# Attention first, weight preparation in stages, and separate runs of experts for even and odd slots

## The chip, the cores and the metric

The kernel runs on one core of a Trainium2 chip. TensorE (PE, with its weight loads as PEld), VectorE (DVE), ScalarE (ACT), GpSimd (POOL) and SyncE (SP, which here only issues transfers) each run their own list of instructions in order and wait for each other by semaphores. A transfer waits in its issuing engine's list like any instruction. The metric is device time in microseconds (us).

## The reference

```python
def reference(x, weight, moe_*, moe2_*):
    # x 4 x 3584 x 192; weight 8 x 7
    w = softmax(weight, axis=-1)                       # seven taps for each of 8 heads
    x = causal_window_sum(x, w)                        # 24 columns a head -> 14336 x 192
    x = moe(x, w_gate, w1, w2)
    return moe2(x, w_gate, w_output_gate, w1, w2)

def moe(x, w_gate, w1, w2):                            # 8 experts, 192 -> 1024 -> 192
    logits = x @ w_gate
    e = argmax(logits, 1); g = softmax(logits)[row, e]
    for each expert: out[e == k] = g * (relu(x[e == k] @ w1[k]) @ w2[k])
```

moe2 is the same with one more factor a row, a sigmoid of x @ w_output_gate at the row's expert. Each row goes to one expert alone, so both layers sort the rows by expert.

## The kernel before

**Attention** (`conv`, L401) takes 128 tiles of 112 rows, four a step, in 32 steps. A step multiplies by a banded matrix (L434, PE), finds a power of two for each row and scales (L447 to L460, DVE), splits the row into two float16 halves (the `chl` tile: L468 on ACT, L469 and L470 on POOL), turns it (L487) for the gate logits (L499) and stores it in DRAM.

**Routing** (`routing`, L1294) takes the logits in groups of 16 tiles, mostly on DVE. After a first wave of groups (`WAVE`: four of eight in layer 1, five of eight in layer 2) it fixes the place of the rows so far (`wave1`), and after the last group that of the others (`wave2`). `Q0` says how many blocks of 128 rows the first wave supplies (42, which is 21 slots).

**Weights** are prepared by `preps` (L238): 8 experts x 2 halves x 2 layers are 32 units. A unit is loaded (L232, L233, L235), its largest magnitude taken by partition (L260, L263, L269), then over all partitions by one `partition_all_reduce` on POOL (L132), it is scaled and rounded on ACT (L295, L296), the remainder taken on POOL (L301, two instructions a unit), and both halves stored in DRAM by SP (L309, L310, L312). Layer 1's units wait for the order of the experts (`eid`), which is taken from the first `EARLY` groups, and stand in that order; no unit comes ahead of that.

**Slots** (`moe`, L1126): each layer has 63, of which 56 are for 256 rows and 7 for 128. A slot belongs to one expert. Its rows are gathered three slots ahead on POOL (L1068), turned by SP (L1076), multiplied by the first weights (L1167, 40 matmuls), passed through ReLU and split (L1169 on ACT, L1170 on DVE) and multiplied by the second weights (L1183, 48 matmuls). Layer 1 splits its result on POOL (`ehl`, L1204 and L1205), turns it (L1212), stores it and takes layer 2's logits (L1221). Layer 2 scatters its rows (L1253). Even and odd slots have a weight buffer each; a load (L1104 to L1107 and L1124) goes out only where the expert differs from the one two slots back. The slots stand in the order of the experts, and so both buffers take every expert in turn.

**The order of the work** is written out in `run` (L1335). Attention steps run alone until `ready` (L1315) finds the first slots' weights and places; the rest are called from the first slots. `Turn` (L1414) hands out routing and preparation in pieces: at points A and B of an attention step and, through `bg2`, of a slot. In one turn a unit is past its all-reduce and the one before it is scaled and has its remainder taken, right behind that all-reduce on POOL.

Of the kernel before, what the change touches and what calls it, by code (L numbers as in the profile page):

```python
# [9 lines left out]
F16 = mybir.dt.float16  # L10
# [21 lines left out]

Q0 = 42
ROUND = 1.5 * 2**23

WAVE = (4, 5)

EARLY = 3
FIRST = 2

PACE = (1, 3, 5, 7)

LEAD = 1

HURRY = 2.0
BUDGET = 1.8

SLOW = 8

GV0 = 4  # L50
GV1 = 4

XACT = 0
W1A = range(8)
NA = 2
LO = ((0, 0, 0, 0, 0, 0, 0, 0), (0, 0, 0, 0, 0, 0, 0, 0))
W2D = (0,)
B2 = 0.3
B3 = 0.1
U2 = 18  # L60
U3 = 62
SLOWS = range(14)
B5 = 0.3
B4 = 1.0
# [4 lines left out]
MODE = 1  # L69
GATE = 9  # L70
GB = 9
LAG = 0
TB = 2
PW1 = 1
PR = 1
PC = 0
Q1 = 0
Q2 = 1
QX = 0
Q2W = 0  # L80
AB = 1.0


class Kern:
    def __init__(self, ctx, tc, x, weight, g1, w11, w12, g2, go2, w21, w22, out):
# [14 lines left out]
        self.parts = 0, Q0 // NSUB, self.NP - 1, self.NS  # L100

        self.full = lambda groups: -(-(groups * JC * CT - E * (T - 1)) // T)
# [5 lines left out]
    def slot(self, u):  # L108


        m, s = divmod(u, self.NS)
        i = s - (self.NP - (E - 1))
        if i >= 0 and i % 2:
            return m, 2, 1 + i // 2, self.NP * NSUB + i // 2, 1
        s -= max(0, i) // 2
        w = max(k for k in range(3) if s >= self.parts[k])
        return m, w, s - self.parts[w], s * NSUB, NSUB
# [43 lines left out]
    def constants(self):  # L161
# [24 lines left out]

        self.run8 = cp.tile([P, E, JC], F32, name="run8")
# [33 lines left out]
    def prep_load(self, m, pos, half):  # L221
# [3 lines left out]
        r = self.wp.tile([P, self.H], F32, tag="r", name="wr")  # L225
        if m == 0:
            ev = nc.sync.value_load(self.eid[pos >= FIRST][0:1, pos : pos + 1], min_val=0, max_val=E - 1)
            w = w[bass.ds(ev, 1)].rearrange("a p f -> (a p) f")
        else:
            w = w[pos]  # L230
# [7 lines left out]
    def preps(self, todo):  # L238
# [6 lines left out]
        todo = [(m, pos, half) for m, pos in todo for half in range(2)]  # L245

        def known(n):
            return n < len(todo) and (todo[n][0] == 1 or (todo[n][1] >= FIRST) in self.eid and (todo[n][1] < GATE or not self.ahead or self.begun >= GB))

        def absmax(u):  # L250
            u.am = wp.tile([P, NA], F32, tag="am", name="wam")
            n = u.what[0] * E + u.what[1]
            u.act = u.what[2] == 0 and n in W1A
            u.max = u.what[2] == 0 or n in W2D
            if u.act:

                ca = H // NA
                for c in range(NA):
                    none = wp.tile([P, CH], F16, tag="none", name="none", bufs=1)
                    nc.scalar.activation(none[:, 0:ca], u.r[:, c * ca : (c + 1) * ca], AF.Abs, scale=2.0**-4, accum_out=u.am[:, c : c + 1])  # L260
            elif u.max:
                for c in range(NC):
                    nc.vector.tensor_reduce(u.am[:, c : c + 1], u.r[:, c * CH : (c + 1) * CH], axis=AX.X, op=ALU.max, apply_absolute_value=True)  # L263
                    yield 0.8
            else:

                for c in range(NC):
                    none = wp.tile([P, CH], F16, tag="none", name="none", bufs=1)
                    nc.scalar.activation(none, u.r[:, c * CH : (c + 1) * CH], AF.Abs, scale=2.0**-11, accum_out=u.am[:, c : c + 1])  # L269

        def scale(u):
            m, pos, half = u.what
            if u.act:
                t = wp.tile([P, 1], F32, tag="amx", name="amx")
                nc.vector.tensor_reduce(t, u.amr, axis=AX.X, op=ALU.max)
                u.amr = t
            else:
                nc.vector.tensor_tensor(u.amr[:, 0:1], u.amr[:, 0:1], u.amr[:, 1:2], ALU.max if u.max else ALU.add)
            s, e = self.pow2(wp, u.amr[:, 0:1], [P, 1], "ws")
            u.h = self.wh.tile([P, 2, H], F16, tag="h", name="wh")  # L280
            if half == 0:
                self.e1 = e
            else:

                nc.vector.tensor_scalar(self.wexp[m][:, pos : pos + 1], self.e1, e, 0.125, ALU.mult, ALU.mult)
            u.direct = LO[half][pos] if m == 0 else 0
            u.s = s

        def main(u, cs):
            for c in cs:  # L290
                q = slice(c * CH, (c + 1) * CH)
                if c < u.direct:
                    nc.scalar.mul(u.h[:, 0, q], u.r[:, q], u.s)
                    continue
# [3 lines left out]
        def rest(u):  # L298
            for c in range(u.direct, NC):
                q = slice(c * CH, (c + 1) * CH)  # L300
                nc.gpsimd.tensor_tensor(u.h[:, 1, q], u.r[:, q], u.h[:, 0, q], ALU.subtract)  # L301
            for c in range(u.direct):
                q = slice(c * CH, (c + 1) * CH)
                nc.vector.scalar_tensor_tensor(u.h[:, 1, q], in0=u.r[:, q], scalar=u.s, in1=u.h[:, 0, q], op0=ALU.mult, op1=ALU.subtract)
# [10 lines left out]
        n = 0  # L315
        new = one = two = None
        while n < len(todo) or new or one or two:
            if not (new or one or two):
                while not known(n):
                    yield "T"  # L320

            yield "A"
            if two:
                store(two)
# [1146 lines left out]
```

## Time and profile before

| | |
|---|---|
| Median of 3 runs | 1713.41 us (1707.09 to 1719.94) |
| Profiled execution | 1707.2 us, span 1705.3 us |
| Mean granted TensorE clock | 0.855 of full speed |
| PE busy | 1277.2 us (75%) |
| DVE busy | 879.8 us (52%) |
| POOL busy | 621.7 us (36%) |
| ACT busy | 553.0 us (32%) |
| DMA | 284.46 MB, mean 167 GB/s |

Times in the views count from the start of the span. Busy time is that of recorded instructions; register, semaphore, configuration and transfer-issuing instructions do not count. Idle time that a row shows as "issue" is time in which the engine waited for nothing that the profile shows. The slots of layer 1 begin at 292 us and those of layer 2 at about 1124 us; stages are told apart by these.

### The profile page before, as it was taken

The page shows a single profiled execution, that of the slowest core. Times are in us where ns is not written, and L with a number is a line of the kernel's source. Part 1 is how long each engine was busy: PE and PEld are TensorE (multiplying, and loading weights), DVE is VectorE, ACT ScalarE, POOL GpSimd, SP SyncE. Part 2 cuts the span into 40 slices and gives each one's busy share as a digit, 9 for nine tenths or more (in the row PEclk, how much of TensorE's full clock was granted, in tenths as well). Part 3 has the DMA queues.
Part 4 walks back from the last instruction along what each step waited for, and adds up shares of the span by engine and source line. Part 5 has one row for each costly group of instructions (what it writes and reads, how often), then busy time and mean ns, then how long its engine had stood idle before and what let it go on. Part 6 is the DMA issues. An engine that isn't in the chain of part 4 may idle for free. (4 is left out here: it accounts for less than half of the span.)

```text
span 1705.3 us, 35513 instructions
## 1 busy us (share of the span) xinstructions
PE 1277.2 (75%) x12456; PEld 1159.7 (68%) x12456; DVE 879.8 (52%) x2639; ACT 553.0 (32%) x989; POOL 621.7 (36%) x689
## 2 busy tenths in 40 slices
PE   2884241756479768868875779889999998989785
PEld 2874241645469657757765668778999998878675
DVE  3795212736547656555645376658755434333232
ACT  0444333333323233424332421232323333233232
POOL 2342233433333333434334242334444443333333
PEclk9675555777779979989988789999999999999988
DMA  3463453965488869777786589885555447876772
GB/s 98 135 155 90 137 138 99 207 174 140 138 183 211 200 181 232 169 196 199 190 196 173 135 223 197 197 197 129 160 147 146 127 109 193 211 200 185 196 206 73
DMA packets 321713, 284.46 MB, mean 167 GB/s; under 512 B 202131, under 2 KB 282188, under 8 KB 321533
## 3 DMA queue, kind: packets, MB, share of 16 engines
q1 hardware_dynamic: 301372, 245.81, 57.1%
q0 software_dynamic: 17136, 34.68, 8.4%
q8 instruction: 102, 1.67, 0.4%
q10 hardware_dynamic: 3024, 1.66, 0.4%
q14 instruction: 79, 0.64, 0.1%
HBM read 273.86 MB, written 60.32 MB: 196 GB/s over the span
## 5 line engine op out<-in xcount | busy, mean ns | idle before, releaser
L1167 PEld LDWEIGHTS <-wb 128*128 128x128 f16 x4840 | 484.3, 105 | 283.0 <-DMA wb<-wda 134.0
L1183 PE MATMUL py<-wb,h 128*128 128x192 f16 x5592 | 498.8, 250 | 52.9 <-DMA wb<-wd 15.4
L1183 PEld LDWEIGHTS <-h 128*128 128x128 f16 x5592 | 476.5, 100 | 64.7 <-issue 41.6
L1167 PE MATMUL ph<-mxt,wb 128*128 128x256 f16 (+1 forms) x2950 | 380.8, 288 | 124.8 <-DMA wb<-wda 90.2
L1170 DVE SCALAR_TENSOR_TENSOR h<-ph,h 128x512 f16<-128x512 f32 x289 | 192.5, 687 | 297.6 <-ACT h L1169 271.5
L1167 PE MATMUL xp<-mxt,wb 128*128 128x256 f16 (+1 forms) x1890 | 247.9, 289 | 58.7 <-DMA wb<-wda 38.6
L1068 POOL DMA_INDIRECT row<-rec,idx x238 | 240.7, 1012 | 69.2 <-issue 50.0
L1253 POOL DMA_INDIRECT out_dram<-o,io x119 | 123.9, 1041 | 297.0 <-ACT h L1169 69.5
L1170 DVE SCALAR_TENSOR_TENSOR h<-xp,h 128x512 f16<-128x512 f32 x187 | 125.7, 687 | 168.1 <-ACT h L1169 143.6
L1169 ACT ACTIVATE h<-ph 128x512 f16<-128x512 f32 x289 | 165.6, 596 | 127.8 <-PE ph L1167 98.2
L301 POOL TENSOR_TENSOR wh<-wr,wh 128x768 f16<-128x768 f32 x64 | 105.6, 1664 | 242.3 <-issue 193.8
L1203 ACT CAST ehl<-exs 128x384 f16<-128x384 f32 (+1 forms) x63 | 31.0, 491 | 349.2 <-DMA rec<-ehl 216.7
L1169 ACT ACTIVATE h<-xp 128x512 f16<-128x512 f32 x187 | 108.9, 596 | 82.2 <-PE xp L1167 56.9
L295 ACT ACTIVATE wr<-wr,wss 128x768 f32<-128x768 f32 x64 | 59.6, 931 | 212.5 <-DVE wss L126 208.0
L1252 ACT ACTIVATE o<-py,sc 128x192 f32<-128x192 f32 x119 | 43.9, 417 | 238.9 <-PE py L1183 130.7
L1204 POOL TENSOR_TENSOR ehl<-exs,ehl 128x256 f16<-128x256 f32 (+1 forms) x63 | 44.0, 698 | 154.1 <-ACT ehl L1203 148.4
L499 PE MATMUL lg<-gawt,cxt 128*112 128x16 f16 x384 | 32.7, 219 | 74.1 <-DVE L L514 49.5
L499 PEld LDWEIGHTS <-cxt 128*112 128x112 f16 x384 | 32.7, 177 | 75.5 <-issue 35.9
L434 PE MATMUL ph<-x,tz 118*112 118x96 f32 x240 | 42.1, 347 | 54.0 <-DMA tz<-td 29.2
L434 PEld LDWEIGHTS ph<-x,tz 118*112 118x112 f32 x240 | 38.0, 251 | 55.9 <-issue 31.5
L434 PE MATMUL xp<-x,tz 118*112 118x96 f32 x272 | 45.4, 345 | 40.5 <-DVE cxs L460 37.0
L434 PEld LDWEIGHTS xp<-x,tz 118*112 118x112 f32 x272 | 42.6, 254 | 41.7 <-DVE cxs L460 37.8
(214 smaller groups left out, 1163.8 us busy)
## 6 DMA issues: line engine op xcount, KB each, us to landing
wb<-wd SPq DMA_DIRECT2D x125, 768.0 KB
wb<-wda SPq DMA_DIRECT2D x125, 512.0 KB
wb<-wdb SPq DMA_DIRECT2D x125, 256.0 KB
wb<-wdb SPq DMA_DIRECT2D x125, 128.0 KB
wr<-in_moe_w_dram SPq DMA_DIRECT2D x16, 768.0 KB
wd<-wh SPq DMA_DIRECT2D x16, 768.0 KB
rec<-chl SPq DMA_DIRECT2D x32, 336.0 KB
rec<-ehl SPq DMA_DIRECT2D x56, 192.0 KB
```

The costliest lines, as they stand in the source:

```text
L295: nc.scalar.mul(u.r[:, q], u.r[:, q], u.s)
L301: nc.gpsimd.tensor_tensor(u.h[:, 1, q], u.r[:, q], u.h[:, 0, q], ALU.subtract)
L434: nc.tensor.matmul(xp[:, :, hh * GD : (hh + 1) * GD], lhsT=self.tz[: self.KI, h, :], rhs=xin[b0][: self.KI, o : o + G, h * GD : (h + 1) * GD],
L499: nc.tensor.matmul(lg[:CT, g, :], lhsT=xt[:, g * 3 + b, :], rhs=self.ga[0][:, 1 if b == 1 else 0].rearrange("p a e -> p (a e)"), start=b == 0,
L1068: nc.gpsimd.indirect_dma_start(out=rw[:, :], out_offset=None, in_=rec[:, :], in_offset=bass.IndirectOffsetOnAxis(ap=idx, axis=0))
L1167: nc.tensor.matmul(ph[:, k, :], lhsT=l, rhs=xt[:, xb, 0:n], start=i == 0, stop=i == 4)
L1169: nc.scalar.activation(hi, ph, AF.Relu)
L1170: nc.vector.scalar_tensor_tensor(lo, in0=ph, scalar=0.0, in1=hi, op0=ALU.max, op1=ALU.subtract)
L1183: nc.tensor.matmul(py[:, c, 0:D], lhsT=h[:, f, a, c * P : (c + 1) * P], rhs=w[:, b, f, :], start=n == 0, stop=n == 3 * NCH - 1)
L1204: nc.gpsimd.tensor_tensor(hl[:, :, D + DB : 2 * D], xs[:, :, 0:P], hl[:, :, 0:P], ALU.subtract)
L1252: nc.scalar.activation(o, py[:, c, 0:D], AF.Copy, scale=sc)
L1253: nc.gpsimd.indirect_dma_start(out=self.out[:, :], out_offset=bass.IndirectOffsetOnAxis(ap=io[:, 0:1], axis=0), in_=o, in_offset=None, bou ...
```

## The change

All 32 attention steps now stand ahead of the first slot (`run` calls `conv` to its end). `WAVE` becomes (6, 5), `EARLY` 4, and `Q0` has a value for each layer: 40 and 56 blocks, 20 and 28 slots. A unit of preparation goes through stages a turn apart: load, one turn of nothing, magnitude, all-reduce and scale factor, rounding and remainder, store; several units are on their way at once. Up to six units of layer 2 go first, while the order of layer 1's experts is not known. `PACE` sets how many turns lie between units. From layer 1's second wave on, and in both waves of layer 2, the even slots take one half of the list of slots and the odd slots the other half (`woven`), so that each buffer goes through its own run of experts; layer 1's first 20 slots stay in the experts' order. The blocks' numbers come from a table `number` instead of a plain count. Transposes of attention tiles are all made by PE, and layer 1's stores all go out from SP.

```diff
--- before.py
+++ after.py
-Q0 = 42
...
-WAVE = (4, 5)
...
-EARLY = 3
-FIRST = 2
...
-PACE = (1, 3, 5, 7)
...
+Q0 = (40, 56)
+
+WAVE = (6, 5)
+
+EARLY = 4
+
+
+PACE = (3, 2, 1, 3)
+
+AHEAD = 6
+
+LA = 2
+
+RAWS = 4
...
+WORK = (0.9, 4.0, 2.2, 0.6)
+FIRST = 20
...
+        last = self.NP - 1
+        ones = list(range(self.NP, self.NS))
+        n = Q0[0] // NSUB
+        mid = (n + last) // 2 + 3
+        odd = list(range(mid, last))
+        for k, at in enumerate((0, 5, 9, 13)):
+            odd.insert(at + k, ones[k])
+        first = list(range(n)) + self.woven(range(n, mid), odd + [last] + ones[4:])
+        n = Q0[1] // NSUB
+        mid = (n + last) // 2 + 3
+        odd = list(range(mid, last))
+        for k, at in enumerate((0, 5, 10)):
+            odd.insert(at + k, ones[1 + k])
+        second = self.woven(range(n // 2), range(n // 2, n)) + self.woven(list(range(n, mid)) + ones[0:1], odd + [last] + ones[4:])
+        self.seq = [self.laid(m, order) for m, order in enumerate((first, second))]
...
+    def woven(a, b):
+        a, b = list(a), list(b)
+        while len(a) > len(b) + 1:
+            b.append(a.pop())
+        while len(b) > len(a):
+            a.append(b.pop())
+        return [x for i in range(len(a)) for x in (a[i : i + 1] + b[i : i + 1])]
...
+        stages = [(load, None)] + [(None, None)] * (LA - 1) + [(absmax, None), (allmax, scale), (main, rest), (store, None)]
+        held = LA + 3
+        self.e1 = [None, None]
+        units, gap = [], 0
+        while any(todo) or units:
             yield "A"
-            if two:
-                store(two)
-            if one:
-                scale(one)
-                if MODE == 0:
-                    main(one, range(NC))
-                elif MODE == 1:
-                    main(one, range(1))
-                yield 0.5
-            if new:
-                yield from absmax(new)
-            yield "B"
-            if one and MODE:
-                main(one, range(1 if MODE == 1 else 0, NC))
-            if new:
-                new.amr = self.allmax(wp, new.am if new.act else new.am[:, 0:NC], NA if new.act else NC, "amr" + "a" * new.act)
-            if one:
-                rest(one)
-            two, one, new = one, new, None
-            if known(n):
-                new = type("Unit", (), {})()
-                new.what = todo[n]
-                new.r = self.prep_load(*todo[n])
-                n += 1
-                if (new.what[0] == 1 and 2 * new.what[1] + new.what[2] in SLOWS) or (new.what[1] >= SLOW and new.what[2]):
-
-                    yield "A"
+            gap -= 1
+
+            m = 0 if todo[0] and self.eid is not None and len(todo[1]) % 2 == 0 else 1
+            more = todo[m] and (m == 0 or not todo[0] or len(todo[1]) > 2 * E - AHEAD or len(todo[1]) % 2)
+            if more and gap <= 0 and sum(u.stage < held for u in units) < RAWS:
+                u = type("Unit", (), {})()
+                u.what, u.stage = todo[m].pop(0), 0
+                units.append(u)
+                gap = PACE[(2 if self.attended else 0) + (m if self.attended else 1 - m)]
+            for point in range(2):
+                for u in units:
+                    do = stages[u.stage][point]
+                    if do:
+                        do(u)
+                        yield 0.2
+                if point == 0:
                     yield "B"
+            for u in units:
+                u.stage += 1
+            units = [u for u in units if u.stage < len(stages)]
...
-            q = k + 1 if self.ahead else k
-            if last < q < NG:
-                attend(q)
-                last = q
+            if k + 1 < NG:
+                attend(k + 1)
...
-            while not self.ready():
-                next(conv, None)
+            while next(conv, "end") != "end":
                 k += 1
                 if k in (8, 10, 12):
                     next(gb, None)
-            for _ in range(LEAD):
-                next(conv, None)
+                self.ready()
+            ctx.close()
+            while not self.ready():
+                bg("B")
+                bg("A")
...
             def bg2(u, point):
-                if point == "A" or u in PACE:
-                    next(conv, None)
                 work.tick("B")
-                work.run(0.5 if u < U2 else B3 if u < U3 else B5)
+                work.run(WORK[2 if u < FIRST else 3])
```

In the order of POOL, `ISA` at the all-reduce's line (L132; L145 in the change) and at the next instruction's line stand for the configuration of the engine, which goes before and after the all-reduce. The first place is attention, eight to ten steps from its beginning. Before, on POOL, steps without any unit (the row subtractions of two steps, and routing's product between them):

```order
L469 TENSOR_TENSOR chl<-cxs,chl 112x4x128
L470 TENSOR_TENSOR chl<-cxs,chl 112x4x64
L606 TENSOR_TENSOR d<-d,inv_110 112x128
L469 TENSOR_TENSOR chl<-cxs,chl 112x4x128
L470 TENSOR_TENSOR chl<-cxs,chl 112x4x64
```

Now, on POOL, the fourth to the seventh step, one unit in three steps:

```order
L145 ISA
L145 ISA amr<-wam 128x2
L477 ISA
L477 TENSOR_TENSOR chl<-cxs,chl 112x4x128
L478 TENSOR_TENSOR chl<-cxs,chl 112x4x64
L435 MEMSET x 6x192
L324 TENSOR_TENSOR wh<-wr,wh 128x768 x2
L477 TENSOR_TENSOR chl<-cxs,chl 112x4x128
L478 TENSOR_TENSOR chl<-cxs,chl 112x4x64
```

Ahead of the first gather of a slot's rows (the `row` tile) POOL had 6 units' all-reduces, 5 units' remainders and 26 steps; now it has 13, 12 and all 32. Of the 32 all-reduces 10 of layer 2's units and 9 of layer 1's stand behind it, where it was 26.

The second place is layer 1's slots, in the middle of the layer. Before, on POOL, two slots, each with its two gathers and the two subtractions of `ehl`; the all-reduce and, right behind it, the remainder `wh` of the unit before follow in the second:

```order
L1068 DMA row_4514<-rec_60,idx_0_2288 128x194
L1068 DMA row_4516<-rec_60,idx_0_2288 128x194
L1204 TENSOR_TENSOR ehl<-exs,ehl 128x2x128
L1205 TENSOR_TENSOR ehl<-exs,ehl 128x2x64
L1068 DMA row_4704<-rec_60,idx_0_2288 128x194
L1068 DMA row_4706<-rec_60,idx_0_2288 128x194
L1204 TENSOR_TENSOR ehl<-exs,ehl 128x2x128
L1205 TENSOR_TENSOR ehl<-exs,ehl 128x2x64
L132 ISA
L132 ISA amr<-wam 128x2
L301 ISA
L301 TENSOR_TENSOR wh<-wr,wh 128x768 x2
```

Now, on POOL, from the all-reduce in one slot to the remainder of the same unit in the next; a third slot without either follows:

```order
L145 ISA
L145 ISA amr<-wam 128x2
L1198 ISA
L1198 TENSOR_TENSOR ehl<-exs,ehl 128x2x128
L1199 TENSOR_TENSOR ehl<-exs,ehl 128x2x64
L1065 DMA row_6311<-rec_60,idx_40_5008 128x194
L1065 DMA row_6313<-rec_60,idx_40_5008 128x194
L1198 TENSOR_TENSOR ehl<-exs,ehl 128x2x128
L1199 TENSOR_TENSOR ehl<-exs,ehl 128x2x64
L324 TENSOR_TENSOR wh<-wr,wh 128x768 x2
```

So an all-reduce stood behind the slot's `ehl` and directly ahead of a remainder; now it stands ahead of the slot's `ehl`, and the remainder comes a slot later. In both, SP's store of a unit is the first thing in the slot behind the remainder, ahead of that slot's weight loads.

## Rows read from the trace of the kernel before

**Rows 1.** The page: span and number of instructions.
```profile
span 1705.3 us, 35513 instructions
```

**Rows 2.** Windows by stage: length, busy us (instructions) by engine, granted clock, DMA share, GB/s.
```profile
35.00:135.00 100.00, 80.06 (x744) 78.09 (x743) 87.09 (x232) 40.17 (x58) 38.05 (x48) 0.70 0.59 149
135.00:294.00 159.00, 52.74 (x426) 50.28 (x426) 49.02 (x184) 58.05 (x91) 41.21 (x42) 0.52 0.42 118
294.00:519.00 225.00, 145.36 (x1262) 126.32 (x1260) 118.83 (x312) 75.97 (x128) 78.67 (x82) 0.78 0.69 167
519.00:956.00 437.00, 341.17 (x3325) 301.37 (x3324) 249.38 (x716) 155.77 (x273) 158.31 (x184) 0.89 0.77 194
956.00:1124.00 168.00, 130.40 (x1365) 117.55 (x1363) 103.03 (x304) 40.51 (x78) 57.92 (x72) 0.86 0.85 190
1124.00:1443.00 319.00, 307.81 (x3169) 288.14 (x3167) 175.84 (x559) 104.21 (x214) 141.64 (x140) 1.00 0.57 146
1443.00:1705.00 262.00, 213.88 (x2150) 192.11 (x2148) 88.26 (x303) 76.20 (x149) 97.91 (x99) 0.93 0.69 181
```

**Rows 3.** The same windows for L1169 alone: four to a slot of 256 rows.
```profile
294.00:519.00 225.00, 26.62 (x49) 0.78 0.69 167
519.00:956.00 437.00, 74.02 (x137) 0.89 0.77 194
```

**Rows 4.** The same two windows for L132, the all-reduce of preparation.
```profile
294.00:519.00 225.00, 3.31 (x9) 0.78 0.69 167
519.00:956.00 437.00, 5.15 (x14) 0.89 0.77 194
```

**Rows 5.** Timeline of POOL, attention steps with preparation: start, length, instruction, [idle before].
```profile
141.66 0.37 POOL L132 PARTITION_ALL_REDUCE amra<-wam  x1 [7.13 <-ACT cxt L492]
156.85 0.37 POOL L132 PARTITION_ALL_REDUCE amr<-wam  x1 [6.12 <-issue]
164.51 3.23 POOL L301 TENSOR_TENSOR wh<-wr,wh 128x768 f16<-128x768 f32 x2 [7.30 <-ACT cxt L492]
251.09 1.30 POOL L1068 DMA_INDIRECT row<-rec,idx  x1 [0.19 <-issue]
286.93 0.37 POOL L132 PARTITION_ALL_REDUCE amr<-wam  x1 [7.60 <-issue]
```

**Rows 6.** Timeline of POOL, attention steps without preparation, and one all-reduce among them.
```profile
43.23 1.15 POOL L469 TENSOR_TENSOR chl<-cxs,chl 112x512 f16<-112x512 f32 x1 [2.12 <-ACT chl L468]
71.07 0.67 POOL L470 TENSOR_TENSOR chl<-cxs,chl 112x256 f16<-112x256 f32 x1
77.72 0.37 POOL L132 PARTITION_ALL_REDUCE gbamr<-gbam  x1 [5.98 <-DVE cat L450]
85.28 1.14 POOL L469 TENSOR_TENSOR chl<-cxs,chl 112x512 f16<-112x512 f32 x1 [7.19 <-issue]
125.22 1.16 POOL L469 TENSOR_TENSOR chl<-cxs,chl 112x512 f16<-112x512 f32 x1 [3.85 <-issue]
```

**Rows 7.** Waits of SP, first layer: who waited for whom, total, times, longest.
```profile
SPq L309 <- POOL wh L301: 72.2, 6, 17.4
SPq L312 <- POOL wh L301: 42.8, 5, 12.0
```

**Rows 8.** Waits of PE, first layer.
```profile
PE ph L1167 <- DMA wb<-wda: 83.1, 16, 12.7
```

**Rows 9.** Timeline of SP at one preparation store.
```profile
958.89 0.35 SPq L312 DMA_DIRECT2D wd<-wh  x1
960.29 0.34 SPq L1104 DMA_DIRECT2D wb<-wda  x1
```

**Rows 10.** Timeline of PE at the same place.
```profile
967.42 0.82 PE L1167 MATMUL xp<-mxt,wb 128*128 128x256 f16 x3 [10.78 <-DMA wb<-wda]
```

**Rows 11.** Lines of PE in 1124 to 1443 us: count | busy, mean ns | idle.
```profile
L1183 PE MATMUL py<-wb,h 128*128 128x192 f16 x1632 | 141.5, 246 | 4.4 <-issue 3.6 <-ACT o L1252 0.7
L1167 PE MATMUL ph<-mxt,wb 128*128 128x256 f16 x832 | 98.8, 273 | 5.1 <-DVE h L1170 1.9 <-DMA wb<-wdb 1.8 <-issue 1.2
```

## What the change is predicted to do

> **What bounds the kernel now.** The first view is the windows by stage: 135 us of attention at a good pace, 159 us in which attention goes on slowly, 830 us for the 63 slots of layer 1 and 581 us for the 63 of layer 2. The reader is to see that PE's share differs: 308 of 319 us in the first part of layer 2, 341 of 437 us in the middle of layer 1, and 53 of 159 us before it [rows 1, 2]. Only 1124 to 1443 us is bounded by PE: 36 slots, 8.9 us each, at the full granted clock of 2.4 GHz. Its matmuls give the same: 40 of 118.8 ns (98.8 us over 832) and 48 of 86.7 ns (141.5 over 1632) are 8.9 us [rows 2, 11].
>
> The second view is POOL's timeline, because POOL is called 36% busy and is not. An all-reduce is recorded with 0.37 us, but POOL stands still for some 6 us ahead of it and 7 us behind it: from 71.74 us (71.07 + 0.67) to 85.28 us, 13.5 us in all, and nothing in between but the all-reduce [rows 6]. A unit of preparation thus holds POOL for 13.5 + 3.2 (the two remainders) = 16.7 us. Where attention steps have a unit each, eight all-reduces start between 141.66 and 286.93 us, 20.75 us apart, while the steps without stand 5.1 us apart (the third at 43.23, the nineteenth at 125.22 us) [rows 5, 6].
>
> The third view is the waits of layer 1. SP waits 115 us for POOL's remainder before it can store a unit [rows 7]; the weight loads stand behind the store. At 958.89 us the store goes out, at 960.29 us the load, and PE, which has nothing to do meanwhile, starts at 967.42 us after 10.78 us of idling [rows 9, 10]. Such waits for first weights make 83.1 us on one of the two sets of banks alone [rows 8].
>
> **The change part by part.** The sum is made against the profiled execution's 1707.2 us (span 1705.3); the median, 1713.41, is 0.4% above it.
>
> *Attention and early units.* Work ahead of the first gather grows from 26 steps, 6 all-reduces and 5 units' remainders to 32, 13 and 12. POOL sets the pace: three steps with one unit are 16.7 + 3 x 1.8 = 22 us there, where DVE at 5.1 us a step needs 15. From the third step at 43 us five such groups end at 153 us. Then seven steps follow with one remaining unit to finish, some 42 us (35 at 5.1 us a step and half of an all-reduce): 195 us. The seventh to tenth all-reduces stand two steps apart, 20.3 us, 61 us in all; then one step, 18.5 us; then two without a step, 33.5 us; and the thirteenth's own 13.5 us: 322 us. Eight gathers of 1.3 us [rows 5], their turning and the first matmuls, 18 us: the first ReLU at 340 us instead of 294, **+46 us**. Below, POOL never idles and each all-reduce takes the shortest form, 5.98 + 0.37 + 6.5 us: 320 us, +26. Above, every unit's turn takes 20.75 us and 23 others 5: 43 + 270 + 115 + 18 = 446 us, +152. I stay near the POOL sum, since the one all-reduce among quick steps [rows 6] was followed by two row subtractions 1.7 us apart: the others had gone on and caught up. The longer tables (`number`) are made ahead of attention's first step on POOL, which waits for PE's banded matrix: 0, and if that cover were gone, a few us that the bounds hold. That PE gets 1.2 GHz in such a stretch, as it does in 135 to 294 us (granted 0.52) [rows 2], costs nothing: its 80.06 us for some 20 steps at 0.70 are 5.4 us a step at 0.52, and three of them still fit in 22 us.
>
> The Trainium skill (GPSIMD Engine Reference, section 2.1, Instruction dispatch) says that the first call to a freshly loaded kernel pays some 6 us of code loading that no instruction shows. The gap ahead of the all-reduce agrees (5.98 us), but the rows show a second, 7.2 us, on the way back. With 6.4 us an all-reduce, an estimate by that page, the front would be some 90 us shorter and the result about 1530; the rows decide.
>
> *Slots 0 to 11 of layer 1*, 225 us: nine all-reduces fall here [rows 4], and nine now. Six steps' row subtractions (11 us of POOL) go, and two of seven weight loads: **-15 us**. Bounds 0 and, if POOL alone counts (9 x 16.7 + 24 gathers of 1.3 us = 182 us), -43.
>
> *Slots 12 to 45*, 437 us [rows 2] with 137 ReLU instructions, four a slot, so 34 slots [rows 3]: 14 all-reduces before [rows 4], 10 now, because six units of layer 2 are already done; 21 weight loads before, 13 now. These loads I counted by going through both lists of slots with the experts that the reference gives each row (72 before in both layers, 51 now). Of the 34 slots three are now short. PE needs 31 x 8.9 + 3 x 4.45 = 289 us. The end of layer 2, which has many loads and no units, takes 251 us without its tail of 11 us, where its 20 long and 7 short slots need 209: 1.2 times. So 347 us, and 8 us for what the units still disturb, as their remainder and store now have a slot more: 355 us, **-82 us**. Above: now 134 us over PE's 303 are 9.6 us a unit; if a unit cost its whole 13.5 us, 289 + 135 = 424 us, -13. Below: 1.1 times PE's need, 318 us, -119.
>
> *Slots 46 to 62*, 168 us: 13 long and 4 short slots instead of 10 and 7, PE's need 133 us; by 1.2, 160 us, **-8 us** (0 to -22). The rest of the seven short slots lies in the stretch above.
>
> *Layer 2*, 581 us: 56 x 8.9 + 7 x 4.45 + 11 = 541 us, so 40 us are waits, nearly all after 1443 us, where 19 loads fall on 27 slots. Now 13 fall on the first 36 slots and 12 on the last 27. That is 0.44 a slot, as in the first 36 slots before (16 loads), which had no waits to speak of: **-35 us** (-10 to -40). Routing of the second wave ends by slot 20 in the order of DVE, ahead of its first use at slot 25; DVE was busy for 55% there (175.84 of 319 us), so it keeps up.
>
> Work moved between slots on ACT and DVE costs nothing: in slots 12 to 45 they are busy for 36% and 57% [rows 2]. With slots of 8.9 us DVE would be late next, where routing falls on it; the factor 1.2 holds room for that. DMA was busy for 336 us of slots 12 to 45 (0.77 of 437) [rows 2]; eight loads and four units less, some 7 us each (an estimate: what the 19 loads after 1443 us add to the share of layer 2's first 36 slots with 16), leave 250 of 355 us, so it does not become the bound.
>
> Sum: 46 - 15 - 82 - 8 - 35 = -94, so 1613 us, and 1620 on the scale of the median.
>
> **The rivals.**
> A. *Everything stands still at an all-reduce.* It now comes ahead of a slot's `ehl` instead of behind it, and SP's turning of `ehl` holds up the second weights and the row turns behind it. In the front the same happens to every turn. For: the 20.75 us turns of 141 to 287 us. Against: the quick recovery at 85 us, and that there each turn also waited for the unit before. Front +152, slots 12 to 45 at 424 us (-13), slots 0 to 11 at 0, the rest as forecast: 152 - 13 - 8 - 35 = +96, about 1809. It decides once the first slot begins after 434 us with the rest as forecast. Chance 0.09.
> B. *The units cease to matter.* Front +26, slots 0 to 11 -30, slots 12 to 45 -119, 46 to 62 -22, layer 2 -38: -183, about 1530. For: only half the unit's chain now lies in one slot. Against: 9.6 us a unit now. Chance 0.13.
> C. *The loads were not the point.* A unit goes on costing 9.6 us through the store's wait, 289 + 96 = 385 us (-52), slots 0 to 11 and 46 to 62 stay, layer 2 gains 10: 46 - 52 - 10 = -16, about 1697. For: 115 us of waits of SP for POOL. Chance 0.16.
>
> **How the numbers follow.** The forecast has 0.62. About 1% is what a measurement of this kernel tells from no change. Faster by more takes in the forecast (0.61), B and nearly half of C: 0.81. Within 1% lie the rest of C and a front halfway to A: 0.11. Slower: nearly all of A, 0.08. The range 1545 to 1705 leaves out A, most of B and C's upper tail, together 0.2.
>
> **What would show it.** Right: POOL's gaps of 6 and 7 us at each of 13 all-reduces ahead of the first slot, that slot's ReLU at 320 to 370 us; SP waiting far less than 115 us at the unit stores; layer 1 below 750 us; layer 2 at 535 to 560 us with PE at the full clock. Wrong: turns of 20 us in attention without a unit's end in them, DVE's `exs` waiting for POOL's `ehl`, or PE waiting as long for first weights as now.

## The result, and the profile after

The changed kernel takes 1638.03 us (median of 4 runs, 1628.8 to 1643.44), the kernel before 1716.6 us in the same comparison: ratio 0.9545, 95% interval 0.9485 to 0.9606. It is faster, 18 us above the 1620 that was forecast and inside the range.

The page of the changed kernel, its span and the busy time of its engines:

```profile
span 1634.9 us, 35772 instructions
PE 1258.3 (77%) x12560; PEld 1162.7 (71%) x12560; DVE 892.6 (55%) x2620; ACT 577.1 (35%) x1037; POOL 624.0 (38%) x709
```

Its windows by stage, columns as in [rows 2]. They are the front up to the first ReLU, slots 0 to 11, 12 to 45 and 46 to 62 of layer 1, and layer 2 in two parts:

```profile
0.00:359.00 359.00, 166.06 (x1407) 159.83 (x1408) 176.68 (x502) 141.24 (x213) 125.59 (x165) 0.62 0.50 133
359.00:562.00 203.00, 143.42 (x1223) 126.54 (x1222) 124.05 (x304) 72.94 (x126) 61.16 (x63) 0.82 0.53 137
562.00:917.00 355.00, 295.08 (x3112) 270.19 (x3112) 219.25 (x630) 141.24 (x258) 149.91 (x179) 0.93 0.78 184
917.00:1062.00 145.00, 135.30 (x1504) 127.29 (x1503) 110.67 (x324) 41.27 (x80) 51.18 (x66) 0.98 0.87 187
1062.00:1393.00 331.00, 315.48 (x3233) 293.21 (x3231) 177.29 (x566) 107.50 (x217) 140.31 (x142) 0.98 0.50 129
1393.00:1635.00 242.00, 202.95 (x2090) 185.60 (x2088) 84.68 (x296) 72.93 (x147) 95.88 (x97) 0.93 0.51 141
```

Read the second number of each row against [rows 2]. The front is 65 us longer; slots 0 to 11 take 203 us instead of 225, slots 12 to 45 take 355 instead of 437, slots 46 to 62 take 145 instead of 168, and layer 2 takes 573 instead of 581. PE's busy time fell by 19 us, from 1277.2 to 1258.3; the rest of the 70 us between the two spans is idle time of PE that went.

POOL's timeline of the changed kernel in the front (start, length, instruction, idle before it) shows why the front grew so far. What follows first is one all-reduce, then a later stretch with two in succession:

```profile
70.21 0.66 POOL L478 TENSOR_TENSOR chl<-cxs,chl 112x256 f16<-112x256 f32 x1
78.18 0.37 POOL L145 PARTITION_ALL_REDUCE amr<-wam  x1 [7.31 <-issue]
86.52 1.15 POOL L477 TENSOR_TENSOR chl<-cxs,chl 112x512 f16<-112x512 f32 x1 [7.97 <-PE lg L504]
...
94.79 0.66 POOL L478 TENSOR_TENSOR chl<-cxs,chl 112x256 f16<-112x256 f32 x1
103.68 0.37 POOL L145 PARTITION_ALL_REDUCE amr<-wam  x1 [8.23 <-DMA rec<-chl]
103.97 0.43 POOL L145 PARTITION_ALL_REDUCE gbamr<-gbam  x1
111.49 1.14 POOL L477 TENSOR_TENSOR chl<-cxs,chl 112x512 f16<-112x512 f32 x1 [7.10 <-ACT cxt L497]
```

From the end of the last subtraction to the next, an all-reduce holds POOL for 15.65 us (70.87 to 86.52), where [rows 6] had 13.5. Two back to back, 0.29 us apart, take 16.0 us together: the price is paid on the way in and on the way out, not by the reduction. From the first subtraction behind the first one (86.52) to the last one ahead of the next (95.45) POOL is never idle, so it does set the pace here.

The waits of the changed kernel in layer 1, 359 to 1062 us (who waited for whom, total, times, longest), first SP's, then PE's:

```profile
SPq L329 <- POOL wh L324: 58.5, 7, 14.0
SPq L332 <- POOL wh L324: 32.0, 4, 11.6
```

```profile
PE py L1180 <- issue: 28.3, 5, 9.3
PE ph L1164 <- DVE h L1167: 23.3, 5, 7.8
PE ph L1164 <- DMA wb<-wda: 11.5, 4, 4.6
```

PE's wait for first weights, 83.1 us in [rows 8], is down to 11.5, although SP still waits 90.5 us at the unit stores (115 in [rows 7]). Another wait of SP fell more. Ahead of a slot's weight loads SP also turns gathered rows, and in slots 12 to 62, where 60.6 of the 83.1 us lay, it waited for the gathers 92.5 us before (519 to 1123 us) and 15.6 us now (562 to 1062 us):

```profile
SPq L1076 <- DMA row<-rec,idx: 92.5, 18, 11.9
```

```profile
SPq L1073 <- DMA row<-rec,idx: 15.6, 10, 3.9
```

At the stores of the same slots it waited 33.9 us before and 25.3 now. PE's longest wait for first weights before, 12.7 us, is such a case. On POOL, SP and PE, one after the other:

```profile
607.27 0.37 POOL L132 PARTITION_ALL_REDUCE amr<-wam  x1 [7.61 <-issue]
615.45 3.24 POOL L301 TENSOR_TENSOR wh<-wr,wh 128x768 f16<-128x768 f32 x2 [7.81 <-issue]
618.87 1.19 POOL L1068 DMA_INDIRECT row<-rec,idx  x1 [0.18 <-issue]
```

```profile
621.68 2.49 SPq L1076 DMA_TRANSPOSE mxt<-row  x2
627.63 0.36 SPq L1104 DMA_DIRECT2D wb<-wda  x1
```

```profile
632.43 0.82 PE L1167 MATMUL ph<-mxt,wb 128*128 128x256 f16 x3 [12.74 <-DMA wb<-wda]
```

The gather stood behind the all-reduce and the remainder, SP's row turn behind the gather (11.9 us of waiting), the load behind the row turn. The change puts the gathers ahead of the all-reduce in POOL's list.

### The profile page after: what moved, and what is told of

The parts are those of the page before. It is cut to its first block, busy times and chain, and to the rows that moved or that the text cites. A ratio compares the mean times of both kernels' runs of the same rounds, so it can differ in the third digit from the quotient of the medians.

```text
span 1634.9 us, 35772 instructions
## 1 busy us (share of the span) xinstructions
PE 1258.3 (77%) x12560; PEld 1162.7 (71%) x12560; DVE 892.6 (55%) x2620; ACT 577.1 (35%) x1037; POOL 624.0 (38%) x709
## 5 line engine op out<-in xcount | busy, mean ns | idle before, releaser
L1164 PEld LDWEIGHTS <-wb 128*128 128x128 f16 x4840 | 470.2, 101 | 187.5 <-issue 70.3
L1164 PE MATMUL ph<-mxt,wb 128*128 128x256 f16 (+1 forms) x2970 | 357.1, 278 | 79.6 <-DVE h L1167 25.3
L1164 PE MATMUL xp<-mxt,wb 128*128 128x256 f16 (+1 forms) x1870 | 235.0, 281 | 33.2 <-DMA wb<-wda 12.0
L306 DVE TENSOR_REDUCE amx<-amr 128x1 f32<-128x2 f32 x32 | 5.0, 155 | 223.6 <-POOL amr L145 223.6
L145 POOL PARTITION_ALL_REDUCE amr<-wam x32 | 11.8, 368 | 227.3 <-issue 166.1
L446 PE MATMUL xp<-x,tz 118*112 118x96 f32 x256 | 49.5, 383 | 43.4 <-DVE cxs L470 40.0
L446 PEld LDWEIGHTS xp<-x,tz 118*112 118x112 f32 x256 | 46.2, 288 | 44.8 <-DVE cxs L470 41.2
```

The lines of the kernel that those rows point to most:

```text
L446: nc.tensor.matmul(xp[:, :, hh * GD : (hh + 1) * GD], lhsT=self.tz[: self.KI, h, :], rhs=xin[b0][: self.KI, o : o + G, h * GD : (h + 1) * GD],
L1164: nc.tensor.matmul(ph[:, k, :], lhsT=l, rhs=xt[:, xb, 0:n], start=i == 0, stop=i == 4)
```

## The experiments

The stages of each profiled run are told apart by the same ReLU instructions in all of them (us, good to about 1; layer 2 up to the span's end). They come from one execution each; e2's took 1647.6 us, 17 less than the median of its runs. The kernel before was run again beside each group of experiments, at medians of 1719.9 to 1722.6 us, and the ratios are to those:

| kernel | first ReLU | slots 0-11 | 12-62 | layer 2 | median, ratio to before [interval] |
|---|---|---|---|---|---|
| before | 294 | 225 | 605 | 581 | 1716.6 |
| changed | 359 | 203 | 500 | 573 | 1638.0, 0.9545 [0.9485, 0.9606] |
| e1 | 359 | 202 | 526 | 579 | 1662.7, 0.9640 [0.9578, 0.9702] |
| e2 | 291 | 205 | 575 | 575 | 1664.2, 0.9674 [0.9622, 0.9725] |
| e3 | 430 | 154 | 576 | 584 | 1746.0, 1.0144 [1.0091, 1.0198] |
| e4 | 263 | 174 | 480 | 570 | 1486.8, 0.8636 [0.8590, 0.8681] |
| e5 | 358 | 203 | 535 | 566 | 1657.7, 0.9626 [0.9574, 0.9678] |
| e6 | 297 | 203 | 528 | 565 | 1594.3, 0.9289 [0.9225, 0.9354] |
| e7 | 237 | 175 | 500 | 563 | 1479.9, 0.8606 [0.8550, 0.8661] |
| e8 | 281 | 172 | 469 | 564 | 1481.5, 0.8598 [0.8552, 0.8645] |
| e9 | 360 | 204 | 502 | 569 | 1633.0, 0.9463 [0.9423, 0.9503] |
| e10 | 361 | 203 | 512 | 571 | 1647.9, 0.9548 [0.9506, 0.9591] |
| e11 | 358 | 203 | 499 | 556 | 1620.6, 0.9415 [0.9366, 0.9463] |
| e12 | 237 | 175 | 505 | 575 | 1493.4, 0.8654 [0.8618, 0.8690] |

Where the order of layer 2's slots is that of the change and its loads are kept, layer 2 takes 563 to 575 us; a difference of a few us in one stage of one profile is within that scatter.

### e1: the changed kernel with the slots in the experts' order

```diff
-        self.seq = [self.laid(m, order) for m, order in enumerate((first, second))]
+        plain = list(range(self.NP - (E - 1)))
+        for k in range(E - 1):
+            plain += [self.NP - (E - 1) + k, ones[k]]
+        self.seq = [self.laid(m, order) for m, order in enumerate((plain, plain))]
```

> The changed kernel with both layers' slots in the plain order of the experts again (72 weight loads instead of 51), all else as changed. If fewer loads are a good part of the gain: layer 1 loses 20 to 40 us and the end of layer 2 some 20 us, so 1675 to 1700 us. If the loads were hidden once the units' stores no longer hold them up: 1638 us, within 8. If they were the whole gain: 1700 to 1720.

1662.7 us: between the cases. Separate runs of experts are worth 25 us of the 79 by the medians and 16 by the two ratios, whose intervals overlap a little; the profiles put 26 in slots 12 to 62 and 6 in layer 2. The rest of the gain is not in the order of the slots. PE's wait for first weights is as small here, with the loads that the kernel before has, as in the changed kernel (561 to 1087 us):

```profile
PE ph L1167 <- DMA wb<-wda: 11.4, 6, 3.4
```

### e2: the kernel before, remainder ahead of the all-reduce

```diff
             yield "B"
...
+            if one:
+                rest(one)
             if new:
                 new.amr = self.allmax(...)
-            if one:
-                rest(one)
```

> The kernel before with one thing moved: in a turn the remainder of the older unit goes out on POOL ahead of the all-reduce of the newer one, so the store a turn later does not stand behind 13.5 us of all-reduce. My theory (the store's wait holds up the weight loads of layer 1): SP's 115 us of waits for the remainder fall below 50, PE's waits for first weights by half, 1655 to 1680 us. The rival (a unit costs what it costs, wherever its remainder stands): 1705 to 1720.

1664.2 us from two lines that change places, inside the range of the theory. In its first layer's slots, 291 to 1071 us, SP waits for POOL's remainder at the stores and PE for the first weights like this:

```profile
SPq L312 <- POOL wh L301: 19.2, 3, 6.7
SPq L309 <- POOL wh L301: 17.0, 3, 6.6
```

```profile
PE ph L1167 <- DMA wb<-wda: 24.9, 9, 5.7
```

SP's 115 us of [rows 7] became 36, and PE's 83.1 us of [rows 8] became 24.9. That bears out the chain of rows 7, 9 and 10: remainder behind an all-reduce, store behind the remainder, load behind the store. But the two lines move more than the remainder. The gathers of the next slot now come straight behind the all-reduce, and the second gap stands behind them:

```profile
638.87 0.37 POOL L132 PARTITION_ALL_REDUCE amr<-wam  x1 [5.77 <-DMA rec<-ehl]
639.43 1.19 POOL L1068 DMA_INDIRECT row<-rec,idx  x1 [0.19 <-issue]
640.92 0.95 POOL L1068 DMA_INDIRECT row<-rec,idx  x1 [0.30 <-issue]
649.36 0.66 POOL L1204 TENSOR_TENSOR ehl<-exs,ehl 128x256 f16<-128x256 f32 x1 [7.50 <-issue]
```

So e2 takes the all-reduce with both gaps out ahead of the remainder, and the second gap out ahead of the gathers. In slots 12 to 62 SP's waits fell from 33.9 to 11.1 us at the stores and from 92.5 to 76.9 us for gathered rows. How the gain divides between the two branches no run shows.

### e3: the kernel before with all attention ahead of the slots

```diff
-LEAD = 1
+LEAD = 10
```

> The kernel before with ten more attention steps ahead of the first slot, so that all 32 precede the slots; preparation, waves and order of slots as before. My theory (attention ahead of the slots earns nothing by itself): the first ReLU 60 to 120 us later, layer 1 shorter by nearly as much, since the units of these turns are done, 1695 to 1735 us. The rival (attention in the slots was what made them slow): below 1690.

1746.0 us, 11 us above the range that was expected. Slots 0 to 11 lose 71 us and slots 12 to 62 lose 29, but the front grows by 136. By the trace it holds three steps more (ACT had split all 32 by the first ReLU, where it was 29) and seven more all-reduces (15 instead of 8). So this is attention moved ahead together with its units, all else as before, and it costs 1.4% (0.9 to 2.0). What attention alone would cost no run shows. The changed kernel's front is not the same one, since it has one unit in three steps at first and 13 in all.

### e4: the changed kernel without the preparation's all-reduces

The largest over the partitions becomes a mean, by a matmul with ones and a factor of 1/128. It goes out at point B, the scaling a turn later.

```diff
-            u.amr = self.allmax(wp, u.am, NC, "amr")
+            a16 = wp.tile([P, NC], F16, tag="a16", name="a16")
+            nc.vector.tensor_copy(a16, u.am)
+            ps = self.rps.tile([P, G, 2 * E], F32, tag="lg", name="aps")[:, 0, 0:NC]
+            nc.tensor.matmul(ps, lhsT=self.ones16, rhs=a16, start=True, stop=True)
+            u.amr = wp.tile([P, NC], F32, tag="amr", name="amr")
+            nc.vector.tensor_scalar(u.amr, ps, 1.0 / P, None, ALU.mult)
...
-        stages = ... [(absmax, None), (allmax, scale), (main, rest), (store, None)]
+        stages = ... [(absmax, None), (None, allmax), (scale_main, rest), (store, None)]
```

> The changed kernel with the 32 all-reduces of preparation taken from POOL: PE adds the 128 partitions' sums with a matrix of ones, DVE takes a 128th (the scale is then the mean over the partitions, where it was the largest). My theory (POOL stands still for 13.5 us at each all-reduce and sets the pace of the front and of slots 0 to 11): the first ReLU at 240 to 280 us instead of 359, slots 0 to 11 in 140 to 170 us instead of 203, 1470 to 1530 us. The rival (the unit's chain over DVE, ACT and SP sets the pace, POOL only lies beside it): above 1600.

1486.8 us, 151 less than the changed kernel and inside the theory's range; only slots 0 to 11, at 174 us, lie above its 140 to 170. 13 all-reduces stood in the front, 8 in slots 0 to 11 and 11 behind; the stages are shorter by 96, 29 and 20 us: 7.4, 3.6 and 1.8 us an all-reduce. (Against e5, which has the same stages, the last is 55 us, or 5.0 each.) POOL's busy time, by contrast, is 617.4 us on this kernel's page and 624.0 on that of the changed one: 6.6 us of busy time stood for 151.

The Trainium skill (GPSIMD Engine Reference, section 4.1, Engine selection) gives a reduction along the partitions to GpSimd. For 128 x 2 values between other work on POOL this case's runs speak against it: with a mean by TensorE in place of the largest value the kernel takes 151 us less, for 32 calls.

### e5: the changed kernel, all-reduce behind `ehl`

The stages of e4 with the all-reduce kept, and the scale factor half a turn later with it: the control for e4's layout, and a test of rival A.

```diff
-        stages = ... [(absmax, None), (allmax, scale), (main, rest), (store, None)]
+        stages = ... [(absmax, None), (None, allmax), (scale_main, rest), (store, None)]
```

> The changed kernel with its all-reduces kept, but each issued at point B of a turn (behind a slot's ehl on POOL) instead of point A, and the scale factor computed in the next turn: the stage layout of e4_sum_on_pe without its replacement of the all-reduces. If e4's 151 us come from the all-reduces themselves: 1638 us, between 1620 and 1655. If the layout did a good part of it: 1600 us or less. If an all-reduce ahead of ehl held up the slots (rival A's mechanism in small): layer 1's slots shorter by 10 to 30 us, 1608 to 1628, with the front unchanged.

1657.7 us, above every case: none had the layout as a loss. So e4's gain is not its layout (against this control it is 171 us). And the all-reduce costs more behind a slot's `ehl` than ahead of it: 20 us by the medians, with intervals that overlap, and 35 us in the profiles' slots 12 to 62 (e9 and e10 repeat this comparison). Rival A had it the other way round. ACT's waits in slots 12 to 45 differ most; first the changed kernel, 562 to 917 us, then e5, 561 to 950 us:

```profile
ACT ehl L1197 <- DVE exs L1193: 75.6, 21, 7.3
ACT ehl L1197 <- DMA rec<-ehl: 63.0, 9, 10.8
```

```profile
ACT ehl L1201 <- DMA rec<-ehl: 114.0, 10, 15.4
ACT wr L318 <- DVE wss L139: 61.2, 11, 9.5
```

ACT stands at a buffer of `ehl` that is not stored yet, and the next slot's ReLU stands behind it. e9 and e10 test this.

### e6: the changed kernel without early units

```diff
-AHEAD = 6
+AHEAD = 0
```

> The changed kernel with AHEAD = 0: the six units of layer 2 that went ahead of the order of the experts now go with the others, in the slots; seven units instead of thirteen begin ahead of the first slot. By e4 an all-reduce costs 7.4 us in the front (96 us for 13) and some 2.7 us in the slots (54 us for 19), so six moved ones give back 28 us, and with the rest of a unit unchanged the time is 1600 to 1620, first ReLU at 300 to 320. By the forecast's own prices (16.7 us of POOL in front, 9.6 us in a slot) 1595, which is not told apart from it. If a unit in the slots costs its whole 13.5 us of POOL or the loads of weights wait for it: 1640 to 1670, with slots 12 to 45 at 400 us or more.

1594.3 us, 44 less, below the 1600 to 1620 and at the forecast's own prices. Its front and the slots behind it, as windows:

```profile
0.00:297.00 297.00, 147.80 (x1405) 142.69 (x1406) 167.34 (x475) 109.70 (x165) 104.96 (x147) 0.67 0.50 129
297.00:500.00 203.00, 142.19 (x1223) 125.23 (x1222) 120.86 (x301) 72.54 (x124) 62.23 (x63) 0.82 0.56 137
500.00:857.00 357.00, 300.93 (x3133) 274.80 (x3131) 228.88 (x636) 148.04 (x270) 152.62 (x180) 0.92 0.80 186
857.00:1028.00 171.00, 141.77 (x1491) 129.11 (x1492) 118.91 (x348) 64.06 (x119) 68.72 (x82) 0.93 0.91 208
```

The front is 62 us shorter, 10.3 us for each of the six units. Slots 12 to 45 take 357 us against 355: five of the six all-reduces now fall on slots 46 to 62, which take 171 us instead of 145, and one on the stretch before. Early units cost more than they bring back.

### e7 and e8: e4 without early units, and e4 with units at a faster pace

```diff
-AHEAD = 6
+AHEAD = 0
```

> e4_sum_on_pe with AHEAD = 0. Without all-reduces a unit in the front takes POOL 3.2 us and DVE and ACT some work that attention also wants. If the front is then set by DVE and not by units: 1480 to 1495 as e4. If units still stretch the front (ACT and DVE busy for 63% and 76% of 135 to 263 us there): first ReLU 20 to 40 us earlier than 263, and the slots take 10 to 20 us more, 1465 to 1480. If the six units are dearer in the slots, where transfers take 0.79 of the DMA engines: 1495 to 1520.

```diff
-PACE = (3, 2, 1, 3)
+PACE = (2, 1, 1, 2)
```

> e4_sum_on_pe with PACE = (2, 1, 1, 2): units go out faster in the front and behind layer 1's units, so more of them are done ahead of the slots. If the front hides them now that no all-reduce holds POOL: slots 12 to 45 shorter by 5 to 15 us and the time 1470 to 1485. If every unit stretches the front as in the changed kernel: first ReLU 10 to 30 us later and 1490 to 1510.

1479.9 and 1481.5 us, not told apart from each other or from e4 by their intervals. In e7 the front is 26 us shorter and slots 12 to 62 are 20 us longer; in e8 it is 18 us longer and they are 11 us shorter. e7 shows its second case's signs and a time on the border of the first two; e8 shows the longer front of its second case and the time of its first. Without all-reduces it hardly matters where the units go. Both are faster than both kernels, by 14% and 9.6%.

### e9 and e10: four buffers for `ehl`, in the changed kernel and in e5

```diff
-            hl = ep.tile([P, NSUB, 2 * D], F16, tag="hl", name="ehl", bufs=2)[:, 0:nq]
+            hl = ep.tile([P, NSUB, 2 * D], F16, tag="hl", name="ehl", bufs=4)[:, 0:nq]
```

> The changed kernel with four buffers instead of two for ehl, layer 1's split result. Between 562 and 917 us ACT waits 63 us for a buffer of ehl to be stored, with the ReLU of the next slot behind it in ACT's list. If that ring carries an all-reduce's stall on POOL to PE: slots 12 to 62 (501 us) shorter by 10 to 40 us, 1600 to 1628. If the stall reaches PE by the stores and loads of weights on SP alone, or not at all: 1638 us within 8.

> e5_allreduce_at_b (1657.7 us) with four buffers for ehl. In e5 ACT waits 114 us of 561 to 950 for a buffer of ehl, against 63 us of the same slots in the changed kernel, and DVE 103 us for ReLU behind it. If this ring is how an all-reduce behind ehl costs 34 us more in slots 12 to 45: most of that comes back, 1615 to 1635. If the 34 us come from the weight loads (PE waits 44 us for first weights there against 19): within 10 us of 1658.

e9, 1633.0 us, is the changed kernel's time: the 63 us of ACT's waits cost nothing there that shows. e10, 1647.9 us, lies between its cases, 10 us below e5 with intervals that overlap; its slots 12 to 62 take 512 us against 535. Against e9, run beside it and different by the place of the all-reduce and of the scale factor alone, e10 takes 15 us more, with intervals apart: the place counts with four buffers too. In e10 PE's waits between 562 and 950 us begin with first weights, as in e5:

```profile
PE ph L1168 <- DMA wb<-wda: 30.3, 4, 10.9
PE pt L649 <- DVE cs L633: 14.2, 2, 12.9
```

So late weights carry a part of what an all-reduce behind `ehl` costs: SP's waits at the unit stores in slots 12 to 62 were 78.7 us in e5, where the changed kernel has 25.3. The ring of two buffers may carry another; these two runs do not settle it.

### e11: layer 2 with hardly any loads

```diff
-            ev = nc.sync.value_load(etab[0:1, 0, o : o + 1], min_val=0, max_val=hi)
+            ov = 0 if m else o
+            ev = nc.sync.value_load(etab[0:1, 0, ov : ov + 1], min_val=0, max_val=hi)
```

> The changed kernel with layer 2 taking the expert of each half's first slot for all slots, so that after the first slots of each half no weights are loaded (its results in layer 2 use the wrong weights). It is the floor that any order of layer 2's slots can reach. By the waits in the trace (PE waits some 18 us for weights in layer 2's 573 us) 1615 to 1627, layer 2 at 550 to 562. If a slot itself takes 8.9 us as the forecast had it, layer 2 would come to 541 us and the time to 1606. If loads slow the gathers and transposes beside them as well: below 1600.

This kernel leaves out nearly all loads of layer 2, which then computes with the wrong weights. 1620.6 us: the first case. Layer 2 takes 556 us as a window of its own:

```profile
1060.00:1616.00 556.00, 514.09 (x5324) 478.55 (x5321) 260.87 (x862) 178.06 (x363) 236.70 (x238) 0.96 0.37 95
```

By this one profile that is about the floor of any order of its slots. The forecast had put 546 us with loads.

### e12: e7 with four buffers for `ehl`

The edit of e9 in e7.

> e7_sum_on_pe_no_early (1479.9 us) with four buffers for ehl. ACT waits 19 + 12 us for a buffer of ehl in slots 12 to 62 there, and PE waits for none of it that shows (its waits are for the sum's own input, 22 + 16 us). If the ring matters only behind an all-reduce: 1480 within 8. If it matters at any slot: 1455 to 1470.

1493.4 us, against 1479.9 of e7: above both cases. There is no gain, and that it is a loss is not shown, as the intervals (0.8618 to 0.8690, 0.8550 to 0.8661) overlap. 12 of the 17 us between the profiles lie in layer 2, which does not use `ehl`; why is open.

## Why the prediction was right, and where its sizes were off

**The front** was forecast at +46 us and measured at +65. The mechanism holds: POOL's gaps stand at all thirteen units, the first ReLU at 359 us is inside the 320 to 370 that was named, and e4's front, without the all-reduces, is 96 us shorter. The term that was mis-sized is the 13.5 us for an all-reduce, from the single one in [rows 6]: in the changed kernel's front it is 13.2 to 17.1 us (without the pair and the last one), 15.65 in the first lines above. The six all-reduces of the three-step groups are one row:

```profile
L145 POOL PARTITION_ALL_REDUCE amr<-wam x6: 367/368/369, 54.2 to 180.3; - x6
```

(180.3 - 54.2) / 5 = 25.2 us a turn, where the forecast had 22; the two-step turns came to 22 us instead of 20.3. The start of attention, put at no cost, is 2.6 us later (the third step's subtraction at 45.85 us instead of 43.23), behind the longer tables. Up to the thirteenth all-reduce this makes 32 us: the forecast's sum stands at 308 us there, and POOL's last remainder ahead of it ended at 340.2. Then 13 us came back, by luck: the forecast had a whole all-reduce and 18 us more to the first ReLU, but the first gather followed the thirteenth after 2.69 us, without the second gap, and the ReLU came at 359.2:

```profile
346.32 0.37 POOL L145 PARTITION_ALL_REDUCE amr<-wam  x1 [6.12 <-issue]
349.39 1.30 POOL L1065 DMA_INDIRECT row<-rec,idx  x1 [2.69 <-DVE cmp L930]
```

**Slots 0 to 11** were forecast at -15 and came to -22. Eight all-reduces lie there instead of nine.

**Slots 12 to 45** were forecast at -82 and came to -82. That the two agree is luck. The factor 1.2 rests on the count of slots that failed in layer 2 (below): by the ReLU instructions the last 27 slots there begin at 1455.5 us and take 239 us without their tail, where the forecast had 251, so the factor is 1.14 and the same sum gives 338 us, -99. The shares, too, are others than the forecast gave. It counted on ten all-reduces instead of 14, on eight loads fewer and on a slot more for remainder and store. Eleven all-reduces came, and the units done ahead gave this stretch nothing (e6: 357 us). What the runs put a size on, for slots 12 to 62 and their 105 us: an all-reduce no longer ahead of the remainder and the gathers (30 us in e2), the all-reduce ahead of `ehl` (35 us in e5), separate runs of experts (26 us in e1), early units (28 us in e6, 26 of them in slots 46 to 62), and attention with its units out of the slots (29 us in e3). These add up to 148, so they overlap, and they are taken from two different kernels; which share each has in the 105 us is not shown.

That SP would wait far less than 115 us at the stores was wrong: 90.5 us, of which 65.2 lie in slots 0 to 11. The third view had named one branch of two. In slots 12 to 62 SP waited 33.9 us at the stores before, and 92.5 us for gathered rows, which the prediction did not count; it is the second that went (15.6 us). Why the stores' waits in slots 0 to 11 do not reach PE, no run shows; PE's own wait row would have been the right sign to name.

**Slots 46 to 62** were forecast at -8 and came to -23. By e6 that is what the early units bring, which the forecast had booked in the stretch before.

**Layer 2** was forecast at -35 and came to -8 here. The step that failed is "36 slots, 8.9 us each" and the 541 us built on it. From 1124 to 1443 us there are 141 ReLU instructions, four a slot, so 35 slots and not 36, and the 1632 matmuls of [rows 11] are 34 slots of 48; by the ReLU instructions the first 36 slots of the kernel before take 332 us, 9.2 each. 56 x 9.2 + 7 x 4.6 + 11 is 558 us, and e11 measured 556. So there were some 25 us of waits to win, not 40. Of these the order won about half: over the runs with the new order and all loads layer 2 takes 568 us on average (nine runs, 563 to 575), over those with the old one (before, e1, e2, e3) 580 (575 to 584). The last window of the changed kernel, 1393 to 1635 us, has new waits in place of some of the old ones:

```profile
PE py L1145 <- ACT o L1247: 7.5, 2, 5.0
PE py L1180 <- ACT o L1247: 5.6, 2, 4.7
```

**The rivals.** A's stall behind `ehl` does not exist in that direction (e5). B was half right about the price: by e4 and e7 it hardly matters where units without all-reduces stand, but the changed kernel keeps its all-reduces. C is refuted as a whole, since slots 12 to 45 came to 355 us and not 385; its doubt about the loads was sound in part, as e1 has 11.4 us of waits for first weights without fewer loads.

The **likeliest case** was right in sign by its mechanism, as the front's price on POOL and the gain in the slots both came. In size it was right partly by luck: two misses, +19 in the front and +27 in layer 2, were met by 7 and 15 us more than forecast in slots 0 to 11 and 46 to 62, slots 12 to 45 came out by a factor that was too large, and the range held the rest. A better version was within reach of the same view: [rows 6] said what an all-reduce costs, and taking it off POOL (e4) gains 151 us more, where all the rearranging around it gained 79.

## What to carry to other kernels

Add up an engine's time by the distance between its neighbours' instructions, not by its busy share: an instruction of 0.37 us held its engine for 13 to 17 here. Ask first whether the costly step can leave the engine, and only then in what order the rest should stand around it; if it has to stay, put what others wait for ahead of it. And count a stage's units by two rows, here ReLU instructions and matmuls, before a time per unit is taken from it.

## What the runs showed of the hardware

Each `PARTITION_ALL_REDUCE` of preparation costs POOL two gaps, every time and not only the first: in the changed kernel 5.7 to 9.2 us ahead of it, and 6.7 to 9.3 us ahead of the next TENSOR_TENSOR behind it. Two in succession cost it once (16.0 us for both). The second gap belongs to the next TENSOR_TENSOR and not to the all-reduce: a MEMSET (130.56 us of the changed kernel) and the gathers of e2 (0.19 us behind) start at once, and the gap stands behind them, 7.72 and 7.50 us.

Both gaps begin with a pair of configuring instructions, which the timeline leaves out. The views of the all-reduce's line in the changed kernel, and of the next subtraction's line from 70 to 90 us:

```profile
L145 POOLq MODIFY_POOL_CONFIG  x66: 1/32/43, 14.8 to 865.2; - x66
```

```profile
L477 POOLq MODIFY_POOL_CONFIG  x2: 83/83/83, 78.5 to 78.5; - x2
```

66 are 33 pairs for 34 all-reduces, since the two in succession share one. The Trainium skill (GPSIMD Engine Reference, section 2.1, Instruction dispatch) has a code load of some 6 us at the first call to a freshly loaded kernel; the shortest gaps ahead, 5.7 us, agree with that size, but the rows show a gap at each return to the all-reduce, and a second one on the way back. What POOL does between the configuring instruction and the next one no row shows.
